# Three homes in turn for the third blocks' left operands, other places for four results, and the next batch's input in four parts

## The chip, the cores and the metric

The kernel runs on one core of a Trainium2 chip. The metric is the time of one execution on the device in microseconds (us); lower is better. The time given is the median of three runs.

## The reference

Routed attention, then a two-layer network with squared ReLU. Cut to what matters:

```python
# q, k, v: (4, 8, 768, 64) float32; centroids: (8, 16, 64)
mask = argmax(q_n . c_n) == argmax(k_n . c_n)          # same cluster
attn = softmax(where(mask, q @ k.T / 8, -1e9)) @ v     # (4, 8, 768, 64)
x = attn.transpose(0, 2, 1, 3).reshape(3072, 512)      # 768 tokens for each of 4 batches
h = x @ w_in                                           # w_in (512, 2048)
g = maximum(h, 0) ** 2
out = g @ w_out                                        # w_out (2048, 512)
```

All is float32. The change touches only the second layer, `g @ w_out`, and the way in which the first layer's input of the next batch is brought in.

## The kernel before

The attention comes first (16 pairs of heads). Then the four batches pass through the network in the order `FEED = (1, 2, 3, 0)`; n = 0 to 3 counts them. Each has an **up** stage (`x @ w_in`, squared) and a **down** stage (`g @ w_out`). From n = 1 on a hand-written order holds on every engine: instructions stand in the engine's queue in the order in which the Python code emits them (`tc.manual_schedule`).

Both layers multiply by the Strassen-Winograd scheme: seven products of half-size blocks in place of eight, with sums and differences of blocks as operands. The products are numbered 1 to 7.

**Up.** `group(i, ...)` forms one of eight groups, seven products of four matmuls each (left 128 columns, right 384). `combine` asks for the products in the order 1, 6, 2, 7, 5, 4, 3. Product 1 needs no sum of x; product 6 needs the sum t2, product 7 needs t3 (which is written over the block `x[0][1]`), product 5 needs t1 and product 4 needs t4. These four sums are made by `x_sums` on VectorE (DVE), from the batch's input `xT` (128 partitions x 3072 floats, 1.5 MB), which for n = 2 and 3 is loaded from the DRAM copy `x_far`. The sums of the weights (`w_sums`, tile `w_s`) are made by GpSimd (POOL), four instructions for each group.

**Down.** A batch's `g` holds 6 blocks of 128 tokens. Four of them (`TWO`) make a full problem for two levels of the scheme. The two others (`THIRD`, the last 128 columns of each half) are half a problem: the third blocks of batch n-1 and of batch n are put side by side, and computed in the down stages of n = 1 and n = 3. Blocks of `g` at `THIRD` are written below as a00, a01 (first half of the tokens) and a10, a11 (second half); each is 128 x 8 x 128. All third blocks and their first-level sums are written to the DRAM tile `g_far` (`store_third`, `third_sums`), and read back by `load_left`.

The class `Down` works through units `(of, j)`: `of` is 0 for the batch's own four blocks, 1 for the pair of third blocks; j is the product of the first level. An odd stage has 14 units, numbered u = 0 to 13:

```
(0,1) (0,4) (1,4) (1,1) (0,5) (1,5) (0,7) (1,7) (0,6) (1,6) (0,2) (1,2) (0,3) (1,3)
```

The even stage (n = 2) has 7, with `of` = 0 only. In each unit:

- `run` issues seven products of the second level (`times`, 8 matmuls of 128x128 each) into two PSUM tiles, `one` and `two`. The right operands are the weights and four precomputed differences in `slot(0..3)`, loaded by `load_right(j)`; each of the four loads waits until TensorE (PE) has read its slot in the unit before.
- `parts` makes, a unit ahead, the sums s and one difference in place (three DVE instructions). A fourth, `sub(x[0][1], x[0][1], s[:, 1])`, stands in the unit itself; the last of the seven products waits for it.
- `combine` turns a unit's products into results, a unit later, in two portions; ScalarE (ACT) copies one product (`copied`). `store` sends finished results to `out` from ACT's DMA queue: results 21 and 22 after product 6, 11 after product 2, 12 after product 3.
- `load_left(j)` brings the third blocks' operands for a later unit, two or four loads of 256 KB on SyncE's (SP) queue.

Where these operands lie is said by `thirds(j)`. Before, j = 4 uses (a01, a11), j = 1 uses (a10, a00), and all the others use (a00, a01) one after the other. The next operands are asked for behind a unit with `of` = 1, for the next such unit. Results lie in tiles of `tp` (`x_t1`, `x_t2`, `x_t4`, those that hold the input's sums in the up stage), in `outp`, and in three pieces of `g` inside a10 and a11 (`third[0..2]`; `third[0]` and `third[1]` are the two halves of a10, `third[2]` the first half of a11). The input of the next batch is loaded whole after unit 1 (`loads()`), and its four sums are made after the last unit (`sums()`), ahead of the last unit's `combine`.

Of the kernel before, what the change touches and what calls it, by code (L numbers as in the profile page):

```python
# [8 lines left out]
F32 = mybir.dt.float32  # L9
# [9 lines left out]
P = 128  # L19
# [6 lines left out]
def kernel(  # L26
# [10 lines left out]
    nc = tc.nc  # L37

    B, H, S, D = q.shape
# [4 lines left out]
    KT = DM // P  # L44
# [21 lines left out]
    loads = att.enter_context(tc.tile_pool(name="loads", bufs=6))  # L66
# [396 lines left out]
    xT = {}  # L463
# [24 lines left out]
    sums = {}  # L488
# [44 lines left out]
    x_far = {b: dram_x.tile([P, KT, S], F32, name=f"x_far{b}") for b in FEED[2:]}  # L533

    H2, F2, M2 = KT // 2, FT // 2, DM // 2

    def sub(out, a, b, eng=nc.vector):
        return eng.tensor_tensor(out=out, in0=a, in1=b, op=ALU.subtract)  # L538

    def x_sums(b):  # L540
        halves = [slice(TB * h, TB * (h + 1)) for h in range(2)]
        x = [[xT[b][:, H2 * g2 : H2 * (g2 + 1), cols] for cols in halves] for g2 in range(2)]
        t1, t2, t4 = (tp.tile([P, H2, TB], F32, name=f"x_t{i}") for i in (1, 2, 4))
        sub(t1, x[0][1], x[0][0])
        yield
        sub(t2, x[1][1], t1)
        yield
        sub(t4, t2, x[1][0])
        yield
        sub(x[0][1], x[1][1], x[0][1])  # L550
        yield x, t1, t2, x[0][1], t4

    def w_sums(i, odd=0):
# [388 lines left out]
    def third_sums(g, n, f):  # L942
        if f < F2 - 1:
            store_third(g, n, f)
        a = block_of(g, f, THIRD)
        third = outp.tile([P, DM], F32, name="third", tag="osb").rearrange("p (j n) -> p j n", j=4)
        plus(third[:, 0], a[1][0], a[1][1])
        sub(third[:, 1], third[:, 0], a[0][0])
        sub(third[:, 2], a[0][0], a[1][0])
        sub(third[:, 3], a[0][1], third[:, 1])  # L950
        return lambda: nc.sync.dma_start(g_far[n][f, :, 3:7], third)

    def times(bank, left, rhs):
        for f in range(F4):
            nc.tensor.matmul(  # L955
                bank, lhsT=left[:, f], rhs=rhs[:, f], start=(f == 0), stop=(f == F4 - 1)
            )

    class Down:
        def __init__(self, b, g, n):  # L960
            self.b, self.g, self.n = b, g, n
# [14 lines left out]

        def thirds(self, j):
            a = blocks(self.g, THIRD)
            return {4: (a[0][1], a[1][1]), 1: (a[1][0], a[0][0])}.get(j, (a[0][0], a[0][1]))

        def load_left(self, j):
            for i, half in ((0, 0), (1, 0), (1, 1), (0, 1)):
# [29 lines left out]
        def find_results(self):  # L1012
            def four(t):
                return t.rearrange("p (i n) -> p i n", i=4)

            def tile(pool, tag):
                return four(pool.tile([P, 4 * P], F32, name="c", tag=tag))

            third = [self.g[:, F4 * i : F4 * (i + 1), 1, THIRD] for i in range(3)]
            if self.n % 2:  # L1020
                self.c = [
                    {11: tile(tp, f"x_t{t}"), 22: third[of]} for of, t in enumerate((1, 2))
                ]
                self.c[0][21], self.c[1][21] = tile(tp, "x_t4"), third[2]
            else:
                self.c = [dict(zip((11, 22, 21), third))]
            for c in self.c:
                c[12] = tile(outp, "osb")
# [35 lines left out]
                    )  # L1064
            self.stores = []

        def run(self, loads, sums):
            first_level(self.g, F2 - 1)
            store_third(self.g, self.n, F2 - 1)
            waiting = None  # L1070
            for u, (of, j) in enumerate(self.units):
                x, s = self.ahead
                y = quarters(right(j))
                copied = spare_tile[:, 4 + u % 2]
                one, two = (
                    bank_tile(4 * P).rearrange("p (i n) -> p i n", i=4) for _ in range(2)
                )
                times(one[:, 0], x[0][0], y[0][0])
                nc.scalar.copy(out=copied, in_=one[:, 0])  # L1079
                self.store()  # L1080
                times(two[:, 0], x[0][1], y[1][0])
                times(two[:, 1], s[:, 1], slot(1))
                times(two[:, 2], x[1][0], slot(2))
                times(two[:, 3], s[:, 0], slot(0))
                times(one[:, 2], x[1][1], slot(3))
                if waiting:
                    next(waiting)
                sub(x[0][1], x[0][1], s[:, 1])
                times(one[:, 1], x[0][1], y[1][1])
                if u + 1 < len(self.units):  # L1090
                    if (k := self.units[u + 1][1]) != j:
# [24 lines left out]

# [74 lines left out]
    x_summed = []  # L1191

    def sum_x(n):
        if n < B:
            x_summed.append(list(x_sums(FEED[n]))[-1])

    for n, b in enumerate(FEED):
        g = gp.tile([P, FT, 2, TB], F32, name="g")
        if n == 0:
            first_up(b, g, Rounding())  # L1200
            first_down(b, g)
            again = nc.values_load(flag[0:1, 0:1], min_val=0, max_val=1)
            with tc.issue_after(last_w_sum[0]):
                sum_x(1)
            manual.enter_context(
                tc.manual_schedule(engines={E.PE, E.DVE, E.Activation, E.Pool, E.SP})
            )
        else:
            stage = Down(b, g, n)
            up(b, g, n, x_summed.pop(), stage.parts)  # L1210
            stage.run(lambda: load_x(n + 1), lambda: sum_x(n + 1))
    manual.close()
    fast.close()

# [189 lines left out]
```

## Time and profile before

| what | value |
|---|---|
| median of 3 runs | 899.92 us (899.64 to 901.14) |
| the profiled execution | 899.35 us |
| its span, first to last instruction | 897.6 us |
| PE busy | 878.8 us, 98% |
| DVE busy | 704.1 us, 78% |
| ACT busy | 389.8 us, 43% |
| POOL busy | 145.7 us, 16% |
| granted TensorE clock | 0.997 |

The stages, from the view of windows (us from the span's start):

| window | stage | PE busy of it |
|---|---|---|
| 516.0 to 606.4 | down, n = 1 | 88.24 of 90.40 |
| 606.4 to 682.7 | up, n = 2 | 73.33 of 76.30 |
| 682.7 to 726.84 | down, n = 2 | 43.16 of 44.14 |
| 726.84 to 801.3 | up, n = 3 | 73.71 of 74.46 |
| 801.3 to 897.6 | down, n = 3, and the end | 87.57 of 96.30 |

In a timeline each row has a start, a duration, the engine, the line, the operation with output <- input, a count, and in brackets the idle time before the row with what ended it. SPq and ACTq are DMA issues. In the chain a row is a start, a duration and what the program's end hung on then.

### The profile page before, as it was taken

The numbers are of one execution on the slowest core, as the hardware profiler recorded it, in microseconds if no ns is written. First come the engines' busy times: TensorE is split into PE (matmuls) and PEld (weight loads), VectorE is DVE, ScalarE is ACT, GpSimd is POOL, SyncE is SP. The second block draws the span as 40 slices with busy tenths as digits, with TensorE's granted clock in tenths as the row PEclk, the third lists the DMA queues.
The fourth block names the chain that finished last, engine by engine and source line by source line (L and its number), as shares of the span: only waits on it lengthen the run. The fifth ranks groups of instructions, "written<-read, shape, count | busy, mean of one in ns | idle before, by whom it ended". The sixth has DMA issues, their size and how long they took to land.

```text
span 897.6 us, 14582 instructions
## 1 busy us (share of the span) xinstructions
PE 878.8 (98%) x5379; PEld 584.6 (65%) x5379; DVE 704.1 (78%) x1271; ACT 389.8 (43%) x621; POOL 145.7 (16%) x168
## 2 busy tenths in 40 slices
PE   9999999999999999999999999998999999999996
PEld 5444444444444455578855599985558975579996
DVE  6798888888888999999566676776667786585875
ACT  5876677776676657630054410003452015530000
POOL 0000100000100257710223100012320052300000
PEclk9999999999999999999999999999999999999998
DMA  6877887777763246236601176662114641126564
GB/s 248 182 188 196 226 239 201 180 210 206 196 147 101 84 164 199 89 106 237 233 35 42 47 231 188 179 180 85 50 53 131 216 142 53 42 71 208 144 188 147
DMA packets 164865, 136.04 MB, mean 152 GB/s; under 512 B 58698, under 2 KB 139186, under 8 KB 164274
## 3 DMA queue, kind: packets, MB, share of 16 engines
q1 hardware_dynamic: 148482, 119.52, 45.5%
q10 hardware_dynamic: 16304, 15.50, 5.6%
q8 instruction: 45, 0.74, 0.3%
q14 instruction: 34, 0.28, 0.1%
HBM read 82.10 MB, written 41.89 MB: 138 GB/s over the span
## 4 chain that ended last, share of the span: by engine, by line
PE 75%; DVE 12%; DMA 9%; issue 2%; SPq 1%; ACT 1%; ACTq 0%; DVEq 0%
PE bank L767 29%; PE sc L441 12%; PE bank L955 9%; PE av_a L475 8%; PE bank L848 5%; DMA g<-g_far 5%; PE av_b L475 4%; PE sc L450 3%; PE sc L329 1%; DVE g L538 1%; DVE l L833 1%; DMA out_dram<-g 1%; DVE spare L833 1%; DVE l L538 1%; PE sc L494 1%
## 5 line engine op out<-in xcount | busy, mean ns | idle before, releaser
L457 ACT ACTIVATE ex<-sc 128x1024 f32<-128x1024 f32 x144 | 144.4, 1026 | 38.3 <-PE sc L441 32.0
L724 DVE TENSOR_TENSOR g<-bank,g 128x384 f32<-128x384 f32 x192 | 102.7, 553 | 72.2 <-PE bank L767 60.4
L441 PE MATMUL sc<-qkT 64*128 64x512 f32 (+1 forms) x768 | 150.6, 484 | 0.0
L743 ACT ACTIVATE g<-g 128x384 f32<-128x384 f32 x122 | 63.3, 519 | 100.3 <-DVE g L724 96.8
L767 PE MATMUL bank<-x_t,w_s 128*128 128x384 f32 x256 | 93.2, 487 | 3.7 <-DVE x_t L538 3.7
L767 PE MATMUL bank<-xT,w_s 128*128 128x384 f32 x256 | 93.4, 487 | 1.1 <-DVE g L724 1.1
L1079 ACT COPY spare<-bank 128x128 f32<-128x128 f32 x35 | 9.3, 265 | 194.6 <-PE bank L955 176.5
L767 PE MATMUL bank<-xT,w_in 128*128 128x384 f32 x256 | 93.3, 487 | 0.0
L441 PEld LDWEIGHTS sc<-qkT 64*128 64x128 f32 x768 | 65.9, 188 | 41.9 <-issue 30.1
L475 PE MATMUL av_a<-ex,v_raw 128*64 128x512 f32 x384 | 85.9, 596 | 0.0
L460 DVE TENSOR_TENSOR total<-total,ex 128x1024 f32<-128x1024 f32 x64 | 78.7, 1229 | 6.5
L558 POOL TENSOR_TENSOR w_s<-w_in 128x256 f32<-128x256 f32 x32 | 26.2, 818 | 325.6 <-PE bank L955 148.9
L955 PE MATMUL bank<-home,l 128*128 128x128 f32 x560 | 74.1, 275 | 1.0 <-DMA home<-w_far 1.0
L767 PEld LDWEIGHTS bank<-x_t,w_s 128*128 128x128 f32 x256 | 48.5, 190 | 38.3 <-issue 3.7
L767 PEld LDWEIGHTS bank<-xT,w_s 128*128 128x128 f32 x256 | 48.3, 190 | 36.1 <-issue 3.3
L767 PEld LDWEIGHTS bank<-xT,w_in 128*128 128x128 f32 x256 | 48.3, 190 | 33.7 <-DVE g L538 0.6
L161 POOL TENSOR_TENSOR w_in<-w_in,w_raw 128x512 int32<-128x512 int32 x16 | 22.0, 1376 | 295.0 <-DVE w_in L153 278.4
L955 PEld LDWEIGHTS bank<-home,l 128*128 128x128 f32 x560 | 68.1, 192 | 1.2 <-DVE g L538 1.1
L744 ACT ACTIVATE g<-g 128x384 f32<-128x384 f32 x122 | 63.8, 523 | 3.9
L475 PEld LDWEIGHTS av_a<-ex,v_raw 128*64 128x64 f32 x384 | 26.1, 137 | 51.0 <-issue 49.3
L450 PE MATMUL sc<-rows 64*128 64x512 bf16 (+1 forms) x360 | 59.0, 323 | 0.3 <-DVE sums_t L503 0.3
L955 PE MATMUL bank<-home,g 128*128 128x128 f32 x416 | 54.9, 275 | 0.0
(181 smaller groups left out, 1401.7 us busy)
## 6 DMA issues: line engine op xcount, KB each, us to landing
home<-w_far SPq DMA_DIRECT2D x92, 256.0 KB
g<-g_far SPq DMA_DIRECT2D x48, 256.0 KB
words<-flat SPq DMA_DIRECT2D x26, 384.0 KB
w_raw<-in_moe_w_in_dram SPq DMA_DIRECT2D x16, 512.0 KB
w_raw<-in_moe_w_out_dram SPq DMA_DIRECT2D x16, 512.0 KB
w_far<-home SPq DMA_DIRECT2D x28, 256.0 KB
v_raw<-in_v_dram SPq DMA_DIRECT2D x16, 384.0 KB
rb<-far_r SPq DMA_DIRECT2D x32, 192.0 KB
```

The source lines that it names most:

```text
L441: nc.tensor.matmul(sc[i][:, e, cols], lhsT=qkT[pair][rows, NCH + c], rhs=qkT[pair][rows, n.start // P : n.stop // P], start=first, stop=no ...
L450: nc.tensor.matmul(sc[i][:, e, cols], lhsT=ohT[pair][rows, 1, c * P : (c + 1) * P], rhs=ohT[pair][rows, 0, columns(i)], start=first, stop= ...
L457: nc.scalar.activation(out=ex[i], in_=sc.pop(i), func=ACT.Exp, scale=SCALE)
L460: eng.tensor_tensor(out=out, in0=a, in1=b, op=ALU.add)
L475: nc.tensor.matmul(bank[D * e : D * (e + 1), 0 : n.stop - n.start], lhsT=raw_v[pair][:, e, c], rhs=ex[i][:, e, cols], start=c == 0, stop=c ...
L558: nc.gpsimd.tensor_tensor(out=s1, in0=a[1][0], in1=a[1][1], op=ALU.add)
L724: nc.vector.tensor_tensor(out=out, in0=bank, in1=to, op=ALU.add)
L743: nc.scalar.activation(out=to, in_=to, func=ACT.Relu)
L744: nc.scalar.square(to, to)
L767: nc.tensor.matmul(bank, lhsT=operands[j][0][:, kk], rhs=operands[j][1][:, kk], start=(kk == 0), stop=(kk == H2 - 1),)
L848: nc.tensor.matmul(bank, lhsT=left[j][:, f], rhs=right(j)[:, f], start=(f == 0), stop=(f == F2 - 1),)
L955: nc.tensor.matmul(bank, lhsT=left[:, f], rhs=rhs[:, f], start=(f == 0), stop=(f == F4 - 1))
```

## The change

- **Homes.** In the odd stages a new tile `extra` (three pieces of 128 x 8 x 128) takes the place of the finished input (tag `x1`). Products 5 and 6 take `extra[0]` and `extra[1]`, products 7 and 2 take a00 and a01, product 3 takes a10 and a11; product 1's loaded half goes to `extra[2]`.
- **Load times.** Operands 4, 1 and 5 are loaded in unit 0; then, behind the units (1,1), (1,5), (1,7) and (1,2), those of products 7, 6, 2 and 3 (`LATER`). Nothing is loaded behind (1,6).
- **Results.** In the odd stages: 11 of the own blocks to `x_t2`, 21 to `third[0]`, 22 to `third[1]`; of the third blocks 11 to `x_t4`, 21 to `x_t1`, 22 to `third[2]`.
- **Input.** The next batch's input comes in four loads of 384 KB (`LOADS`): in the even stage behind the units 1 to 4, in an odd stage behind the units 9, 10 (two) and 12.
- **Sums.** The order of the sums is t1, t2, t3, t4 (t3 and t4 change places). t1 is made behind the last unit but one, t2 and t3 behind the last, t4 after the last `combine`.

```diff
@@ x_sums
         sub(t2, x[1][1], t1)
         yield
+        sub(x[0][1], x[1][1], x[0][1])
+        yield
         sub(t4, t2, x[1][0])
-        yield
-        sub(x[0][1], x[1][1], x[0][1])
         yield x, t1, t2, x[0][1], t4
@@ ahead of class Down
+    LATER = {1: 7, 5: 6, 7: 2, 2: 3}
+    LOADS = ({1: (0,), 2: (1,), 3: (2,), 4: (3,)}, {9: (0,), 10: (1, 2), 12: (3,)})
@@ Down.thirds
-            return {4: (a[0][1], a[1][1]), 1: (a[1][0], a[0][0])}.get(j, (a[0][0], a[0][1]))
+            return {
+                4: (a[0][1], a[1][1]), 1: (self.extra[:, 2], a[0][0]), 3: (a[1][0], a[1][1]),
+                7: (a[0][0], a[0][1]), 2: (a[0][0], a[0][1]),
+            }.get(j, (self.extra[:, 0], self.extra[:, 1]))
@@ Down.find_results
                 self.c = [
-                    {11: tile(tp, f"x_t{t}"), 22: third[of]} for of, t in enumerate((1, 2))
+                    {11: tile(tp, "x_t2"), 21: third[0], 22: third[1]},
+                    {11: tile(tp, "x_t4"), 21: tile(tp, "x_t1"), 22: third[2]},
                 ]
-                self.c[0][21], self.c[1][21] = tile(tp, "x_t4"), third[2]
+                self.extra = xp.tile([P, 3, F2, P], F32, name="extra", tag="x1")
@@ Down.run
-                    if of and j != 4 and (k := next((k for o, k in self.units[u + 1 :] if o), None)):
-                        self.load_left(k)
+                    if of and j in LATER:
+                        self.load_left(LATER[j])
...
                 if u == 0:
                     store = third_sums(self.g, self.n, F2 - 1)
+                    self.find_results()
                     if self.n % 2:
                         self.load_left(4)
+                        self.load_left(1)
                     store()
                     if self.n % 2:
-                        self.load_left(1)
-                    self.find_results()
-                elif u == 1:
-                    loads()
+                        self.load_left(5)
                 if waiting:
                     next(waiting, None)
                 waiting = self.combine(of, j, one, two, copied)
-                if u + 1 == len(self.units):
-                    sums()
+                to_end = len(self.units) - 1 - u
+                for kk in LOADS[self.n % 2].get(u, ()):
+                    load_x(self.n + 1, kk)
+                if to_end == 1:
+                    sum_x(self.n + 1, 1)
+                elif to_end == 0:
+                    sum_x(self.n + 1, 2)
             list(waiting)
+            sum_x(self.n + 1, 1)
             self.store()
@@ load_x, sum_x
-    def load_x(n):
+    def load_x(n, kk):
         if n < B:
-            xT[FEED[n]] = xp.tile([P, KT, S], F32, name="xT", tag="x1")
-            nc.sync.dma_start(xT[FEED[n]], x_far[FEED[n]])
+            b = FEED[n]
+            if b not in xT:
+                xT[b] = xp.tile([P, KT, S], F32, name="xT", tag="x1")
+            nc.sync.dma_start(xT[b][:, kk], x_far[b][:, kk])
...
-    def sum_x(n):
+    def sum_x(n, steps):
         if n < B:
-            x_summed.append(list(x_sums(FEED[n]))[-1])
+            if n not in x_summed:
+                x_summed[n] = [x_sums(FEED[n])]
+            for _ in range(steps):
+                x_summed[n].append(next(x_summed[n][0]))
```

For the first batch, before the hand-written order begins, all four sums are still made at once, in the new order.

More of the change, by code (lines that the diff above doesn't have):

```diff
@@ L1065, in store, with run @@
             self.stores = []
-        def run(self, loads, sums):
+        def run(self):
             first_level(self.g, F2 - 1)
@@ L1184 @@
     wtp = spare_tile = four_r = None
-    def load_x(n):
+    def load_x(n, kk):
         if n < B:
-            xT[FEED[n]] = xp.tile([P, KT, S], F32, name="xT", tag="x1")
-            nc.sync.dma_start(xT[FEED[n]], x_far[FEED[n]])
-    x_summed = []
-    def sum_x(n):
+            b = FEED[n]
+            if b not in xT:
+                xT[b] = xp.tile([P, KT, S], F32, name="xT", tag="x1")
+            nc.sync.dma_start(xT[b][:, kk], x_far[b][:, kk])
+    x_summed = {}
+    def sum_x(n, steps):
         if n < B:
-            x_summed.append(list(x_sums(FEED[n]))[-1])
+            if n not in x_summed:
+                x_summed[n] = [x_sums(FEED[n])]
+            for _ in range(steps):
+                x_summed[n].append(next(x_summed[n][0]))
     for n, b in enumerate(FEED):
@@ L1203 @@
             with tc.issue_after(last_w_sum[0]):
-                sum_x(1)
+                sum_x(1, 4)
             manual.enter_context(
@@ L1209 @@
             stage = Down(b, g, n)
-            up(b, g, n, x_summed.pop(), stage.parts)
-            stage.run(lambda: load_x(n + 1), lambda: sum_x(n + 1))
+            up(b, g, n, x_summed.pop(n)[-1], stage.parts)
+            stage.run()
     manual.close()
```

## The prediction

> **What bounds it now.** The page first: PE is busy 878.8 us of a span of 897.6, so at most 18.8 us are to be had, start and end included. I then read PE's waits, PE's timeline for the rows with an idle time in brackets, and for each of them DVE's and SP's timelines and the chain. PE's waits:
>
> ```profile
> PE bank L767 <- DVE x_t L538: 3.7, 2, 3.0
> PE bank L955 <- DVE g L538: 2.4, 2, 1.3
> ...
> PE bank L955 <- DMA home<-w_far: 1.0, 1, 1.0
> PE bank L955 <- DMA g<-g_far: 0.9, 2, 0.6
> ```
>
> All of these lie where the change works: the input's sums (L538 into x_t), the third blocks' operands (g), and a slot load (home) that stands behind the whole input in SP's queue. PE's timeline places them, four in the first odd stage, two in the even one, two in the last:
>
> ```profile
> 585.92 1.13 PE L955 MATMUL bank<-w_out,g 128*128 128x128 f32 x8 [0.30 <-DMA g<-g_far]
> ...
> 591.91 1.16 PE L955 MATMUL bank<-w_out,g 128*128 128x128 f32 x8 [1.29 <-DVE g L538]
> ...
> 600.78 1.13 PE L955 MATMUL bank<-w_out,g 128*128 128x128 f32 x8 [0.57 <-DMA g<-g_far]
> ...
> 610.83 1.53 PE L767 MATMUL bank<-x_t,w_s 128*128 128x384 f32 x4 [2.97 <-DVE x_t L538]
> ...
> 703.54 1.13 PE L955 MATMUL bank<-home,l 128*128 128x128 f32 x8 [0.98 <-DMA home<-w_far]
> ...
> 729.05 1.53 PE L767 MATMUL bank<-x_t,w_s 128*128 128x384 f32 x4 [0.75 <-DVE x_t L538]
> ...
> 876.05 1.16 PE L955 MATMUL bank<-w_out,g 128*128 128x128 f32 x8 [1.08 <-DVE g L538]
> ...
> 884.78 1.13 PE L955 MATMUL bank<-w_out,g 128*128 128x128 f32 x8 [0.42 <-SPq L1215]
> ```
>
> The second is DVE being late, and DVE is late because it waited for operands; the third is the same for the last operands; the fourth is t2, whose place x_t2 is still being stored:
>
> ```profile
> 571.60 0.69 DVE L833 TENSOR_TENSOR l<-g 128x512 f32<-128x512 f32 x1 [3.12 <-DMA g<-g_far]
> ...
> 585.00 0.69 DVE L833 TENSOR_TENSOR l<-g 128x512 f32<-128x512 f32 x1 [1.84 <-DMA g<-g_far]
> ...
> 599.85 1.20 DVE L833 TENSOR_TENSOR l<-g 128x512 f32<-128x512 f32 x1 [3.29 <-DMA g<-g_far]
> ...
> 609.72 0.96 DVE L538 TENSOR_TENSOR x_t<-xT,x_t 128x768 f32<-128x768 f32 x1 [2.56 <-DMA out_dram<-c]
> ```
>
> The chain says what the operands of product 3 hung on: a store of results, then SP's issue, then the load.
>
> ```profile
> 589.31 5.91 DMA out_dram<-g
> 595.24 0.37 SPq L985
> ...
> 595.66 4.17 DMA g<-g_far
> ```
>
> **What the Trainium skill says.** "GPSIMD Engine Reference", section Specifications: POOL's SBUF interfaces are shared with DVE, and contend with DVE instructions that have two SBUF inputs. The trace agrees: beside POOL's w_s sums (719.10 to 723.2) four 512-element adds took 1.07, 1.10, 1.21 and 1.10 us, alone 0.69; adds with a PSUM input stay at 0.42. "DMA: Bandwidth & Descriptors", section Queues, rings and completion order: SP's and ACT's DMAs share the same 16 engines, each serving the queues in turn. The trace agrees: with stores in the same microseconds a load landed 6.2 us after issue (877.92 to 884.09), with few of them 4.2. The same page, section Anatomy of one DMA: a DMA's wait is served on the issuing engine, so what stands behind it in that queue waits too; SP's four issues of 592.60 took 4.19 us, two behind a wait, where a free four take 2.03.
>
> **The change, stage by stage.** A unit is 56 matmuls in 6.25 us (starts 0.893 apart per product); T11 is the start of unit 11, and so on.
>
> *n = 1.* T11 is 584.56. Without waits T12 = 590.81, T13 = 597.06, up starts at 603.31. Before it started at 606.40, and its product 6 at 610.83 in place of one product (1.29) later, 607.69. To be had: 3.1 + 3.1 = 6.2 us.
>
> Operands 5, 7, 6 and 2 now come one third-block unit earlier: 2, issued at 578.0 to 580.2 and landed at 585.0, will be issued behind unit 7, at 565.5, where operands 6 were (landed at 571.6). DVE no longer waits at 571.60 and 585.00. Followed through its queue, bounded by PE (the sub of unit 9 can start 1.99 us after T9 = 572.06, as in unit 1), product 6's combine ends at 586.5 instead of 590.06, the sub of unit 11 at 588.2, and PE wants it at T11 + 5.36 = 589.9. Cover 1.7 us, so 0.30 and 1.29 go.
>
> Operands 3 are late next. Their new home (a10, a11) holds results that must have been stored. These stores were issued at 588.84 to 591.5; now, with the combine 3.6 us earlier, at 586.0 to 587.9, ahead of the slot loads instead of among them. The chain has such stores at 3.60 us (874.31) and 5.91 (589.31), the longer among other loads; I take the shorter, so 591.5 for the last. SP issues the slot loads at 587.5 to 590.2 (PE sets them) and the four operand loads at 590.6 to 592.5; at 4.2 to 4.9 us they land at about 597, the third of them (which DVE wants first) at 596.3. PE needs the last at T13 + 0.89 = 597.95. So 0.57 goes.
>
> But DVE now has t1 between. From 596.3: parts 1.93, plus about 0.8 beside POOL's first group of sums, which starts at T12 + 4.5 = 595.3; the rest of a combine 1.1; t1 1.03; the next combine's first portion 1.12; the sub 0.6: 602.9. PE wants it at T13 + 5.36 = 602.42, so about 0.6 us of wait, a new one. Behind it DVE does 1.0 of combine, then t2 (1.0 to 1.36 beside POOL): 605.0 to 605.4. Up starts at 603.9, product 6 wants t2 at 605.2. Its place x_t2 is free: result 11 of the own blocks is stored a unit earlier. Product 6 starts at 605.4. t3 and t4 (by 606.7 and 610.2, the last combine between) are wanted at 607.9 and 610.5. **Gain 610.83 - 605.4 = 5.4 us.** Bounds: 6.2 if POOL costs nothing; 2.9 if operands 3 land as late as before (599.85 + 5.8 of DVE + 0.9 + 1.3 = 607.9).
>
> *The input's loads.* Four issues in place of one, 0.4 to 0.5 us each on SP. The first waits in SP's queue for PE to leave unit 9 (`extra` is read until 578.3); behind it stand only the next two and the slot loads of unit 11, which wait for PE until 587.5 anyway: nothing. The fourth stands behind operands 3 and ahead of slots that are wanted 75 us later: nothing. In units 9 and 10, 1.1 MB of input take the place of 1 MB of operands 2. If the engines ran full, operands 3 would land up to 1 us later; that is in the range. In unit 0, 1 MB of operands 5 takes the place of 1.5 MB of input, behind operands 4 and 1: nothing.
>
> *n = 2.* The wait at 703.54 exists because 1.5 MB stand between two units' slot loads (issued at 694.03). With 384 KB there the first slot lands near 700, wanted at 702.4: **1.2 us** with the restart. At the end, before: product 6 began 0.9 late, and another 0.3 us of small waits on x_t3 and PSUM. Now t1 is in the unit before. DVE there is full: the combine of product 6 ends 3.12 us after T6 (beside POOL), t1 1.03, then 1.12 and 0.6: 5.95, and PE wants the sub at 5.36: 0.64 us of new wait; t2 is then in time by about 0.1. **Net 0.5**, between -0.6 (both sums at 1.4) and 1.2. Together 1.7.
>
> *n = 3.* No next input. As in n = 1, waits of 1.08 and 0.42, with restarts and two rows of 0.1 to 0.2 in units 9 and 11, come to 2.2 us of PE; operands 3 land at about 880.5 with T13 = 881.7, 1.4 early. Then the tail: before, DVE ended at 892.3, 2 us behind PE (about 890.3), its queue still late from 884.09. Now PE ends at 888.1, and only the last 128x256 add (0.42) with its wait follows: 888.8. The two stores and the end follow as before. **Gain 3.5 us**; 0 if operands 3 land as before.
>
> *n = 0.* The order of t3 and t4 changes; PE has no wait there: nothing.
>
> Sum: 5.4 + 1.7 + 3.5 = 10.6 us. The profiled execution took 899.35 (span 897.6 and 1.75 around it), 0.57 below the median; a difference carries over, so 899.92 - 10.6 = **889.3 us**. All that is to be had, 6.2 + 2.5 + 3.7, would give 887.5.
>
> **Rivals.** *The last operands stay late* (chance 0.17). For it: the load chain of a store, an issue and 4 to 6 us; the input in units 9 and 10 fills the DMA engines. Against: the stores leave 3 us earlier. Then 2.9 + 1.2 + 0 = 4.1 us of gain: 895.8. *No early operands* (0.04): if `extra` or the new place of results is tied to a later event than I read, SP's in-order queue gives the early loads back; about 899.9. *The store ahead of operands 3 decides* (0.05), the slower side: product 3's operands overwrite results, so they can't leave before these stores have landed. With s us from the last store's issue (587.9; in n = 3 872.7) to its landing, 0.5 for the next issue and 4.2 for the load, the third load lands at 592.6 + s, and up's product 6 follows 9.1 later: n = 1 gains 9.1 - s, n = 3 6.7 - s, n = 2 its 1.7. The change is slower from s = 8.8 on; the slowest store seen took 5.9. With s = 11: 904.4.
>
> **Numbers.** The forecast has 0.74. Below 0.2% (1.8 us, about what a measurement can tell from no change) nothing counts as faster. The forecast and the late operands are faster: 0.91; no early operands 0.04 the same; the slower rival 0.05. The range 887.3 to 894.5 holds the forecast's bounds and reaches towards the late operands.
>
> **What would show it.** Right: no operand wait on DVE at units 8 and 10; one left before unit 13's parts, ending near 596.5; product 6 of up near 605.4; no wait on home<-w_far; new PE waits of 0.5 to 1 us on the sub of the last unit in n = 1 and 2; DVE's last add within 1 us of PE's end. Wrong: operands 3 landing after 599, or waits on l<-g in earlier units.

## The result, and the profile after

The changed kernel takes 891.42 us (median of 6 runs, 889.51 to 893.32), the kernel before 899.78 beside it (6 runs): a ratio of 0.9907, with a 95% interval of 0.9889 to 0.9924. The gain is 8.4 us; 10.6 were forecast, and the time lies 2.1 above the predicted 889.3, inside the range. The profiled execution took 891.05 us, its span is 889.3, and the granted clock 0.997 as before. One run of n3_early_sums_first (below) took 915.07 us, in a slow state with a granted clock of 0.948, and is left out of its median and ratio.

The page's first lines, after:

```profile
span 889.3 us, 14583 instructions
...
PE 876.6 (99%) x5379; PEld 584.1 (66%) x5379; DVE 703.8 (79%) x1271; ACT 389.9 (44%) x621; POOL 145.7 (16%) x168
```

PE has the same number of matmuls, and of the 8.3 us of span 6.1 were PE's idle time (18.8 before, 12.7 now). The other 2.2 are in its busy time (878.8 before), in part because the first matmuls behind a wait are longer in PE's timeline (1.13 to 1.16 us for eight, where 1.06 is usual) and there are fewer waits now. PE's waits after (us in total, times, the longest):

```profile
PE bank L955 <- DMA g<-g_far: 1.1, 2, 0.8
...
PE bank L955 <- DVE g L538: 0.4, 1, 0.4
...
PE bank L955 <- DVE home L538: 0.3, 1, 0.3
```

The wait on x_t (3.7) and the one on home<-w_far (1.0) are gone, the one on DVE's g went from 2.4 to 0.4; the last operands (g<-g_far) still cost PE 1.1 (0.9 before), and the sub of the last unit in n = 2 is new. PE's timeline places what is left:

```profile
598.58 1.13 PE L955 MATMUL bank<-w_out,g 128*128 128x128 f32 x8 [0.80 <-DMA g<-g_far]
...
603.65 1.16 PE L955 MATMUL bank<-w_out,g 128*128 128x128 f32 x8 [0.37 <-DVE g L538]
604.65 1.46 PE L767 MATMUL bank<-xT,w_in 128*128 128x384 f32 x4
605.94 1.45 PE L767 MATMUL bank<-x_t,w_s 128*128 128x384 f32 x4
...
720.23 1.16 PE L955 MATMUL bank<-w_out,home 128*128 128x128 f32 x8 [0.30 <-DVE home L538]
...
722.52 1.45 PE L767 MATMUL bank<-x_t,w_s 128*128 128x384 f32 x4
...
876.15 1.13 PE L955 MATMUL bank<-w_out,g 128*128 128x128 f32 x8 [0.33 <-DMA g<-g_far]
...
880.69 1.06 PE L955 MATMUL bank<-w_out,g 128*128 128x128 f32 x8
```

605.94 and 722.52 are product 6 of the up stages; neither row has a bracket now. These two rows cut the gain into parts that can be set against the prediction's. With the first matmul of the down stage n = 1 at 515.78 before and 515.43 after:

| stretch | before | after | gain |
|---|---|---|---|
| start to down n = 1 | 515.78 | 515.43 | 0.35 |
| to product 6 of up, n = 2 | 95.05 | 90.51 | 4.54 |
| to product 6 of up, n = 3 | 118.22 | 116.58 | 1.64 |
| to the end of the span | 168.55 | 166.78 | 1.77 |
| sum | 897.6 | 889.3 | 8.30 |

DVE's rows at the units where it waited for operands before (571.60, 585.00, 599.85), then the first row of the last unit's parts in n = 3 and DVE's last row:

```profile
568.05 0.69 DVE L833 TENSOR_TENSOR l<-extra 128x512 f32<-128x512 f32 x1
...
581.07 0.69 DVE L833 TENSOR_TENSOR l<-g 128x512 f32<-128x512 f32 x1
...
597.69 0.93 DVE L833 TENSOR_TENSOR l<-g 128x512 f32<-128x512 f32 x1 [4.54 <-DMA g<-g_far]
...
875.49 0.69 DVE L833 TENSOR_TENSOR l<-g 128x512 f32<-128x512 f32 x1 [4.30 <-DMA g<-g_far]
...
883.29 0.42 DVE L833 TENSOR_TENSOR c<-bank,c 128x256 f32<-128x256 f32 x1
```

The first two have no bracket: the early homes do what they should. The third and the fourth wait longer than any before, since DVE arrives early at operands that have not come. That alone is no loss (DVE waits longer here than before, and both stages are shorter all the same); what it costs is on PE, 0.80 and 0.33, and at the end: DVE's last add ends at 883.71, PE's last matmul at 881.75, so DVE still stands 2 us behind PE as it did before.

The chain, after, at both places (start, duration, what the end hung on):

```profile
591.61 5.99 DMA g<-g_far
...
869.20 6.19 DMA g<-g_far
```

Before, the load in this place took 4.17 in n = 1 and 6.08 in n = 3. The prediction took 4.2 to 4.9 in n = 1; this is the main number of it that fell, and the experiments go after it.

### The profile page after: what moved, and what is told of

Its sections match the earlier page's. It is cut to its first block, busy times and chain, and to the rows that moved or that the text cites. A ratio compares the mean times of both kernels' runs of the same rounds, so it can differ in the third digit from the quotient of the medians.

```text
span 889.3 us, 14583 instructions
## 1 busy us (share of the span) xinstructions
PE 876.6 (99%) x5379; PEld 584.1 (66%) x5379; DVE 703.8 (79%) x1271; ACT 389.9 (44%) x621; POOL 145.7 (16%) x168
## 4 chain that ended last, share of the span: by engine, by line
PE 85%; DVE 9%; DMA 3%; issue 2%; ACT 1%; SPq 0%; ACTq 0%; DVEq 0%
PE bank L767 30%; PE bank L955 18%; PE sc L441 12%; PE av_a L475 8%; PE bank L848 5%; PE av_b L475 4%; PE sc L450 3%; PE sc L329 1%; DMA g<-g_far 1%; DVE spare L833 1%; DVE c L833 1%; PE sc L494 1%; DMA qkT<-words 1%; DVE g L724 1%; DVE g L538 1%
## 5 line engine op out<-in xcount | busy, mean ns | idle before, releaser
L767 PE MATMUL bank<-x_t,w_in 128*128 128x384 f32 x128 | 46.5, 486 | 0.0
```

Source lines behind the costliest of these rows:

```text
L767: nc.tensor.matmul(bank, lhsT=operands[j][0][:, kk], rhs=operands[j][1][:, kk], start=(kk == 0), stop=(kk == H2 - 1),)
```

## The experiments

For all of them, lengths of the stages from PE's timeline, from the start of the first matmul to the end of the last, in us. D1, D2, D3 are the down stages of n = 1, 2, 3; U2 and U3 the up stages between; the tail is from PE's last matmul to the end of the span. Free of waits an odd down stage takes 87.71 and an up stage 72.41 (the shortest seen).

| kernel | D1 | U2 | D2 | U3 | D3 | tail | median us | ratio to before, 95% interval |
|---|---|---|---|---|---|---|---|---|
| before | 90.79 | 75.61 | 45.15 | 73.73 | 89.97 | 7.2 | 899.78 | |
| changed | 89.38 | 72.41 | 44.50 | 72.41 | 88.28 | 7.5 | 891.42 | 0.9907 (0.9889 to 0.9924) |
| homes_only | 88.70 | 73.81 | 48.34 | 73.72 | 88.76 | 7.4 | 894.15 | 0.9934 (0.9913 to 0.9955) |
| input_only | 90.49 | 73.84 | 44.50 | 72.41 | 90.39 | 6.9 | 897.88 | 0.9979 (0.9969 to 0.9989) |
| ops3_early | 90.05 | 72.41 | 44.50 | 72.41 | 87.71 | 5.8 | 890.06 | 0.9896 (0.9875 to 0.9917) |
| even_whole | 89.38 | 72.41 | 44.97 | 72.41 | 88.96 | 6.3 | 892.86 | 0.9927 (0.9905 to 0.9949) |
| after_again | 89.11 | 72.41 | 44.51 | 72.41 | 88.51 | 7.6 | 891.33 | 0.9906 (0.9878 to 0.9935) |
| n3_early_sums_first | 88.74 | 73.43 | 43.93 | 73.33 | 87.71 | 6.0 | 889.87 | 0.9897 (0.9862 to 0.9931) |
| no_slots3 | 88.95 | 72.41 | 44.51 | 72.41 | 87.71 | 6.0 | 889.58 | 0.9886 (0.9857 to 0.9915) |
| even_whole_2 | 89.11 | 72.41 | 45.74 | 72.40 | 88.03 | 7.8 | 892.61 | 0.9921 (0.9892 to 0.9951) |
| n3_early | 89.38 | 72.41 | 44.51 | 72.41 | 87.71 | 6.0 | 889.96 | 0.9900 (0.9882 to 0.9918) |
| n3_early_n1_one | 89.75 | 72.41 | 44.51 | 72.41 | 87.71 | 5.9 | 890.06 | 0.9896 (0.9879 to 0.9913) |

The first four experiments ran beside one set of runs of the kernel before (median 899.34), the next four beside another (899.33), the last two beside a third (899.28). All edits are against the changed kernel.

### The homes alone (homes_only)

The homes, load times and places of results stay; the input comes whole and its sums are made at the end, in the old order.

```diff
...
-    LOADS = ({1: (0,), 2: (1,), 3: (2,), 4: (3,)}, {9: (0,), 10: (1, 2), 12: (3,)})
+    LOADS = ({1: (slice(0, KT),)}, {9: (slice(0, KT),)})
...
-                if to_end == 1:
-                    sum_x(self.n + 1, 1)
-                elif to_end == 0:
-                    sum_x(self.n + 1, 2)
+                if to_end == 0:
+                    sum_x(self.n + 1, 4)
             list(waiting)
-            sum_x(self.n + 1, 1)
```

> The new homes, the new places of the results and the new load times alone; the input comes whole (behind unit 1 in the even stage, behind unit 9 in the odd one, since its place holds the operands until then) and its four sums are made behind the last unit in the old order. My theory: the homes carry the odd stages' gain (4.5 us in n = 1 and 1.8 in n = 3 by the two profiles), the input in parts and the early sums only that of n = 2 (1.6). So this runs at about 893.0 us, with the wait on home<-w_far (about 1.0 us) back in n = 2 and operand waits gone from units 8 and 10. Rival: the sums' new place frees t2 in n = 1 (the wait of 2.97 us before), and the homes only remove 0.3 and 1.3 us twice: then about 896.

Measured: 894.15, a gain of 5.2, where the theory had 893.0 and the rival 896. The profiled execution (897.91) was the slowest of its seven runs, so its stages are read for their waits and not added up. PE's timeline:

```profile
606.80 1.53 PE L767 MATMUL bank<-x_t,w_s 128*128 128x384 f32 x4 [0.84 <-DVE x_t L538]
...
701.39 1.77 PE L955 MATMUL bank<-home,l 128*128 128x128 f32 x8 [2.55 <-DMA home<-w_far]
...
728.52 1.53 PE L767 MATMUL bank<-x_t,w_s 128*128 128x384 f32 x4 [0.74 <-DVE x_t L538]
```

D1 is 2.09 shorter than before, more than in the changed kernel (1.41): here t1 doesn't stand ahead of the last unit's sub, and PE doesn't wait for that. Of the 2.97 us that PE waited for x_t in n = 1, 0.84 are left although the sums stand where they stood. So the homes and the places of the results alone take most of that wait: DVE is less late from the operands, and its row of t2 has no wait for the store out of x_t2 any more (2.56 before). The next experiment shows that the sums alone take as much of U2 (1.8 us in both). The two parts overlap, and their gains don't add up. The waits of n = 2 stay: they are the input's part.

### The input alone (input_only)

The four parts and the new sums stay (in the odd stages the loads stand behind units 1 to 4, since `extra` is not there); homes, load times and results are as before.

```diff
-    LOADS = ({1: (0,), 2: (1,), 3: (2,), 4: (3,)}, {9: (0,), 10: (1, 2), 12: (3,)})
+    LOADS = ({1: (0,), 2: (1,), 3: (2,), 4: (3,)},) * 2
...
+            return {4: (a[0][1], a[1][1]), 1: (a[1][0], a[0][0])}.get(j, (a[0][0], a[0][1]))
...
-                    if of and j in LATER:
-                        self.load_left(LATER[j])
+                    if of and j != 4 and (k := next((k for o, k in self.units[u + 1 :] if o), None)):
+                        self.load_left(k)
...
```

> The old homes and old places of results; the input in four parts (behind units 1 to 4 in every stage) and its sums in the new order and at the new places. My theory: in n = 1 t2 still waits for the store of result 11 of the third blocks, whose place it takes, so nothing is gained there; n = 2 gains 1.6 us: about 898.2 us, with PE's wait on x_t in n = 1 still near 3 us. Rival: the earlier sums bring most of the change's gain: 894 or less.

Measured: 897.88, a gain of 1.5. PE's timeline:

```profile
592.30 1.16 PE L955 MATMUL bank<-w_out,g 128*128 128x128 f32 x8 [1.03 <-DVE g L538]
...
609.80 1.53 PE L767 MATMUL bank<-x_t,w_s 128*128 128x384 f32 x4 [1.20 <-DVE x_t L538]
...
873.73 1.16 PE L955 MATMUL bank<-w_out,g 128*128 128x128 f32 x8 [1.60 <-DVE g L538]
```

The total came as expected, one detail didn't: the wait on x_t in n = 1 fell to 1.20 where I expected it to stay near 3. U2 is 1.8 shorter with the new order and places of the sums alone; t2 still waits for the store out of its place, 1.54 us for 2.56. PE's waits on DVE at the operands stay (1.03 and 1.60 for 1.29 and 1.08), and the last unit's sub in n = 1 has a new one of 0.80. D2 and U3 have the changed kernel's lengths, so what n = 2 gained comes from the input's part, and what n = 3 gained from the homes (D3 and tail 97.3 here, 97.2 before).

### The last operands earlier, in both odd stages (ops3_early)

Of product 3's four operand loads three are asked for behind unit 10, ahead of the slot loads; only the one whose place is stored last stays where it was.

```diff
-        def load_left(self, j):
-            for i, half in ((0, 0), (1, 0), (1, 1), (0, 1)):
+        def load_left(self, j, which=((0, 0), (1, 0), (1, 1), (0, 1))):
+            for i, half in which:
...
-                        self.load_left(LATER[j])
+                        self.load_left(LATER[j], *[((1, 0),)] * (LATER[j] == 3))
...
+                if self.n % 2 and u == 10:
+                    self.load_left(3, ((1, 1), (0, 0), (0, 1)))
```

> The changed kernel, with three of the four loads of product 3's operands issued behind unit 10, ahead of unit 12's slot loads; only the one that overwrites the third blocks' result 22 stays behind them. My theory: what is left in n = 1 and 3 hangs on the landing of these operands (DVE waits for them until 597.69 in n = 1 and 875.49 in n = 3, 6 us after issue, since they queue behind 1 MB of slot loads). With 0.25 MB left there they land some 3 us earlier, PE's waits of 0.80, 0.37 and 0.33 go, and DVE's last add ends within 1 us of PE: 3 us less, about 888.4. Rival 1: DVE's work in the last units bounds them anyway: within 0.5 us of 891.4. Rival 2: SP's queue, now waiting for the stores of unit 8's results ahead of the slot loads, delays those: a new wait on home<-w_far and 892 or more.

Measured: 890.06, a gain of 1.4 for the 3 expected. In n = 3 all came: D3 is 87.71 with no wait, the tail 5.8. In n = 1 the load's place was paid for by another wait. SP's timeline, then PE's:

```profile
580.03 7.10 SPq L993 DMA_DIRECT2D g<-g_far  x3
587.18 5.44 SPq L914 DMA_DIRECT2D home<-w_far  x4
```

```profile
593.04 1.13 PE L955 MATMUL bank<-home,l 128*128 128x128 f32 x8 [0.97 <-DMA home<-w_far]
...
603.98 1.16 PE L955 MATMUL bank<-w_out,g 128*128 128x128 f32 x8 [0.87 <-DVE g L538]
```

The trace has 16 completion signals for each DMA, and it has landed with the last. Two of the three loads wait for stores: those issued at 579.20 and 580.54 landed at 585.15 and 586.70, and SP goes on at 585.17 and 586.72. So the three issues take SP 7.10 us, and the third operand load goes out at 586.77, just ahead of the slots. The first slot load, at 587.18, is hardly later than in the changed kernel (587.09), but the operands stand ahead of it, the last of them until 592.24. It lands at 592.91, 5.73 us after its issue where the changed kernel has 3.65, and PE waits 0.97 for it. (The four slot issues take 5.44 us for 3.00 because the fourth goes out at 592.30 only, behind the landing of the third operand load: the two signal on the same semaphore.) D1 is 0.67 longer than in the changed kernel. In n = 3 the same loads stand in the same order and cost nothing: the store that the third load waits for took 2.86 us there (6.16 in n = 1), and all three had landed at 865.30, ahead of the first slot load (865.46). There is no next input beside them in n = 3; that this is the reason wasn't tested.

### The even stage's input whole again (even_whole, even_whole_2)

```diff
-    LOADS = ({1: (0,), 2: (1,), 3: (2,), 4: (3,)}, {9: (0,), 10: (1, 2), 12: (3,)})
+    LOADS = ({1: (slice(0, KT),)}, {9: (0,), 10: (1, 2), 12: (3,)})
```

> The changed kernel with the input whole behind unit 1 in the even stage (n = 2), in parts as before in the odd one. My theory: the wait on home<-w_far at unit 3 of n = 2 (0.98 us, 1.2 with the restart) comes back: about 892.6. Rival: it does not, since the wait belonged to something else in the old order: 891.4.

> The input whole behind unit 1 of the even stage, once more, beside the changed kernel on the same chip. In the first run PE's wait on home<-w_far in n = 2 was 0.23 us, in the kernel with the homes alone 2.55, in the kernel before 0.98: the wait depends on the execution. If the four parts are worth their 1.2 us, this is slower than the changed kernel by 0.5 to 2 us; if not, by under 0.3.

Measured: 892.86 and, with the changed kernel beside it on the same chip (891.33), 892.61, so 1.3 us for the four parts in n = 2, against the 1.2 of the prediction. The intervals of the ratios overlap; the stage is clearer. D2 is 44.97 and 45.74 where the changed kernel has 44.50 and 44.51, and PE's timeline of the second has the old wait back:

```profile
698.64 1.13 PE L955 MATMUL bank<-home,l 128*128 128x128 f32 x8 [1.00 <-DMA home<-w_far]
```

The size of this wait varies between executions: 0.23 and 1.00 in two of this same kernel, 0.98 before and 2.55 in homes_only, where the input also comes whole behind unit 1.

### The changed kernel again (after_again)

No edit.

> The changed kernel once more, beside the others of this group on the same chip: 891.4 us, 0.99 of the kernel before.

Measured: 891.33. In this execution the third load of n = 1 landed 1.2 us sooner than in the first one: at 596.42, 4.74 us after its issue, with the same loads ahead of it. By the completion signals 0.9 of that is the last signal alone: the fifteenth came at 596.40 here and at 596.69 in the first execution, the sixteenth at 596.42 and 597.60. DVE's timeline shows what the earlier landing is worth:

```profile
596.51 1.27 DVE L833 TENSOR_TENSOR l<-g 128x512 f32<-128x512 f32 x1 [3.53 <-DMA g<-g_far]
597.82 1.10 DVE L538 TENSOR_TENSOR l<-l,g 128x512 f32<-128x512 f32 x1
```

The first two operations of the parts take 1.27 and 1.10, where the first execution had 0.93 and 0.69: they now run beside POOL's first group of sums (595.01 to 598.36 here, 595.18 to 598.07 in the first execution). This is the contention that the Trainium skill describes ("GPSIMD Engine Reference", section Specifications), and which the prediction priced at 0.8 us in all. D1 is shorter by 0.27 only.

### The last operands earlier in n = 3 alone, and t1, t2 and t3 behind the last sub (n3_early_sums_first)

In n = 3 the loads as in ops3_early; t1, t2 and t3 are made behind the last unit's own sub, so that t1 no longer stands ahead of it.

```diff
...
-                        self.load_left(LATER[j])
+                        early = self.n == B - 1 and LATER[j] == 3
+                        self.load_left(LATER[j], *[((1, 0),)] * early)
...
+                if u + 1 == len(self.units):
+                    sum_x(self.n + 1, 3)
                 if waiting:
...
-                if to_end == 1:
-                    sum_x(self.n + 1, 1)
-                elif to_end == 0:
-                    sum_x(self.n + 1, 2)
+                if self.n == B - 1 and u == 10:
+                    self.load_left(3, ((1, 1), (0, 0), (0, 1)))
```

> The changed kernel with two further edits: three of the four loads of product 3's operands behind unit 10 in n = 3 alone (in n = 1 the slots came late by it), and t1, t2 and t3 in the last unit, behind the sub that PE waits for and ahead of the rest of the combine of the unit before. My theory: in n = 3 2.3 us less, as in the run with the early loads in both stages; the new waits of 0.37 us in n = 1 and 0.30 us in n = 2 are the price of t1 ahead of that sub, so they go, and t2 is still in time (by 0.7 us, or just if POOL's sums slow it): 0.5 and 0.4 us less. Together about 3 us under the changed kernel, 888.2. Rival: t1 and t2 behind the sub are late for up's product 6, which then waits as long as the sub did: only n = 3 gains, 889.1.

Measured: 889.87, the rival's 889.1 rather than the theory's 888.2. The waits on the sub are gone (D1 0.64 shorter, D2 0.57), and come back a few us later in the up stages, 1.0 and 0.9 longer. PE's timeline:

```profile
611.17 1.53 PE L767 MATMUL bank<-x_t,w_in 128*128 128x384 f32 x4 [0.41 <-DVE x_t L538]
...
728.11 1.53 PE L767 MATMUL bank<-x_t,w_in 128*128 128x384 f32 x4 [0.42 <-DVE x_t L538]
```

Product 4 now waits for t4. DVE's timeline has no free time between the last operands and t4, so this order of its work moved the wait and didn't remove it.

### Without the slot loads of product 3 (no_slots3)

The four slot loads of product 3 are left out in the odd stages, so the last two units multiply by the slots of product 2. The kernel leaves out part of the computation, and serves only to time the loads behind.

```diff
-                    if (k := self.units[u + 1][1]) != j:
+                    if (k := self.units[u + 1][1]) != j and not (self.n % 2 and k == 3):
                         load_right(k)
```

> The changed kernel without the four slot loads of product 3 in the odd stages, which leaves out part of the computation: units 12 and 13 of n = 1 and 3 multiply by product 2's differences instead. It measures what the 1 MB of slot loads ahead of operands 3 costs their landing. SP then issues the operands as soon as the stores of unit 9's results have landed. My theory: these stores land near 590 (n = 1), so the issue moves little, by about 1 us, but the landing comes 4.2 us after the issue, not 6.1: DVE starts near 595 instead of 597.7 in n = 1, and near 872.5 instead of 875.5 in n = 3, and n = 3 gains its 2.3 us. Rival: the landing is long because of the operands' own 512-byte pieces and the stores on ACT's queue, and the slots don't matter: landing 6 us after issue still, gain under 1 us.

Measured: 889.58. In n = 3 the operands come before DVE asks (its row has no bracket), D3 is 87.71 and the tail 6.0. In n = 1 the third load lands 4.0 us after its issue; the chain, SP's timeline and DVE's:

```profile
593.41 4.01 DMA g<-g_far
```

```profile
588.02 6.50 SPq L993 DMA_DIRECT2D g<-g_far  x4
```

```profile
597.51 0.98 DVE L833 TENSOR_TENSOR l<-g 128x512 f32<-128x512 f32 x1 [3.14 <-DMA g<-g_far]
...
871.98 0.69 DVE L833 TENSOR_TENSOR l<-g 128x512 f32<-128x512 f32 x1
```

Yet the landing is hardly earlier than in the changed kernel (597.42 for 597.60): SP's four issues take 6.50 us, because the second waits for a store. The trace's completion signals give both times: the last signal of the store issued at 588.86 comes at 592.87, and SP goes on at 592.88. So with the slots out of the way the store is what the last operands of n = 1 hang on, 4.0 us of it; the theory, which had DVE start near 595 in n = 1, missed that (597.51).

The same signals show where the changed kernel's 6 us go:

| us | last slot load landed | operand loads landed | third load: issued, took |
|---|---|---|---|
| before, n = 1 | 595.04 | 596.63, 598.63, 599.83, 600.65 | 595.66, 4.17 |
| before, n = 3 | 880.75 | 881.61, 882.55, 884.00, 884.64 | 877.92, 6.08 |
| changed, n = 1 | 593.30 | 594.74, 596.10, 597.60, 598.44 | 591.61, 5.99 |
| changed, n = 3 | 871.01 | 872.72, 874.44, 875.39, 876.01 | 869.20, 6.19 |
| no_slots3, n = 1 | none | (one gone early) 596.23, 597.42, 598.26 | 593.41, 4.01 |

Loads of SP's queue land one behind the other, about 1.2 us apart. The Trainium skill ("DMA: Bandwidth & Descriptors", section Queues, rings and completion order) says that each engine takes a queue's descriptors in ring order, though not that they complete in that order; in the table they landed in order in every row. The time from issue to landing is then mostly not the load's own: it is what stands ahead of it.

The rival is ACT's stores in the same microseconds. The view of the DMA queues tells the two apart, over the time from the third load's issue to its landing. The time of a queue is its share of the 16 engines times this window:

| third load | window us | SP's queue: MB, share, time | ACT's queue: MB, share, time |
|---|---|---|---|
| before, n = 1 | 4.17 | 0.82, 67.8%, 2.8 us | 0.26, 19.1%, 0.8 us |
| before, n = 3 | 6.08 | 1.18, 68.9%, 4.2 us | 0.25, 12.6%, 0.8 us |
| changed, n = 1 | 5.99 | 1.58, 83.8%, 5.0 us | 0.26, 12.7%, 0.8 us |
| changed, n = 3 | 6.19 | 1.40, 75.2%, 4.7 us | 0.26, 12.3%, 0.8 us |
| after_again, n = 1 | 4.74 | 1.23, 88.2%, 4.2 us | 0.26, 16.2%, 0.8 us |
| no_slots3, n = 1 | 4.01 | 0.81, 70.4%, 2.8 us | 0.26, 20.1%, 0.8 us |
| n3_early (below), the one load left, n = 3 | 3.50 | 0.44, 39.6%, 1.4 us | 0.26, 22.6%, 0.8 us |

The stores take the same 0.8 us in every row. What differs is SP's own queue. (Its share can include loads behind the third one, where an engine was ahead of the others.)

### The last operands earlier in n = 3 alone (n3_early)

n3_early_sums_first without its move of the sums: in n = 3 three loads behind unit 10, all else as in the changed kernel.

```diff
+                        early = self.n == B - 1 and LATER[j] == 3
+                        self.load_left(LATER[j], *[((1, 0),)] * early)
...
+                if self.n == B - 1 and u == 10:
+                    self.load_left(3, ((1, 1), (0, 0), (0, 1)))
```

> The changed kernel with three of the four loads of product 3's operands behind unit 10, ahead of the slot loads, in n = 3 alone; the sums stay where the change put them. My theory: n = 3 loses its wait on operands (0.3 to 0.6 us) and DVE ends within 1 us of PE, 2.3 us less; n = 1 and 2 as in the changed kernel: 889.1. Rival: nothing beyond the 1.3 us that the two earlier kernels with such loads showed in the median, 890.0, since part of what DVE saves is lost in the last stores.

Measured: 889.96. D1 to U3 are the changed kernel's, D3 is 87.71 and the tail 6.0. The chain and DVE's timeline in n = 3:

```profile
865.67 4.21 DMA out_dram<-g
...
869.96 3.50 DMA g<-g_far
```

```profile
873.49 0.69 DVE L833 TENSOR_TENSOR l<-g 128x512 f32<-128x512 f32 x1 [2.45 <-DMA g<-g_far]
...
881.39 0.42 DVE L833 TENSOR_TENSOR c<-bank,c 128x256 f32<-128x256 f32 x1
```

The one load left hangs on a store (4.21) and then takes 3.50, with slots ahead of it but no other operands. DVE's last add now ends 0.8 us behind PE (881.81, PE 881.03). Against the changed kernel it is 1.4 us lower in the medians, of other runs, and the intervals overlap: the whole time is the rival's 890.0 and not the theory's 889.1. The stage is clear (0.6, and 1.5 us of tail), and so over all traces: D3 and the tail together take 95.3 to 96.2 us in the five executions with these loads as the change has them (changed, after_again, homes_only, even_whole, even_whole_2) and 93.5 to 93.8 in the five where they come earlier or have no slots ahead.

### And one of the loads earlier in n = 1 (n3_early_n1_one)

```diff
+                        late = [((1, 0),)] if self.n == B - 1 else [((0, 0), (1, 0), (0, 1))]
+                        self.load_left(LATER[j], *late * (LATER[j] == 3))
...
+                if self.n % 2 and u == 10:
+                    self.load_left(3, ((1, 1), (0, 0), (0, 1))[: 3 if self.n == B - 1 else 1])
```

> The same, and in n = 1 the one load that overwrites no result (second half of a11) behind unit 10, the three others behind the slots. My theory: 0.25 MB less behind the slots, so n = 1's operands land about 0.9 us earlier, PE's wait on them (0.2 to 0.8 us) goes; but DVE's sums then fall beside POOL's first group and cost up to 1 us more, so the sub of the last unit gains little: 0.3 us under n3_early, 888.8. Rival: the engines are full with the input's three parts at that time, so the load pushes the slots of unit 12: a wait on home<-w_far, and 0.5 us over n3_early.

Measured: 890.06, no gain; a miss. PE's wait for the operands in n = 1 is gone, and D1 is 0.37 longer all the same. PE's timeline:

```profile
595.23 1.16 PE L955 MATMUL bank<-home,l 128*128 128x128 f32 x8 [0.18 <-DMA home<-w_far]
...
604.87 1.16 PE L955 MATMUL bank<-w_out,g 128*128 128x128 f32 x8 [0.60 <-DVE g L538]
```

A slot is late now, as the rival said, and the sub later than before. In n = 1 the stores, the slots, the operands and the input share the same 10 us, and three orders of the loads gave three places of the wait with D1 between 89.1 and 90.1.

## Why the prediction was right, and where it was off

- **n = 1, the early operands: right.** The rows at 568.05 and 581.07 have no bracket. The combine of product 6 ended at 586.1 (586.5 forecast), its stores were issued by 587.5 (587.9), and SP issued the four operand loads from 590.19 to 592.66 (590.6 to 592.5). The forecast used the clock of the kernel before, and the stage began 0.35 earlier here, so in the stage's own time these came as forecast.
- **n = 1, the last operands: mis-sized.** The third load was to land at 596.3, "at 4.2 to 4.9 us" after its issue. It took 5.99 and landed at 597.60, in the stage's own time 1.65 later than forecast. This is the term that was wrong. The 4.2 came from a load whose slots had landed when it was issued (595.04, then 595.66, in the table), with two operand loads ahead; now three of the four slot loads were still under way at its issue (591.61) beside the two operand loads. The prediction had the other row, 877.92 to 884.09, in hand, and read it as "with stores in the same microseconds", the 4.2 as "with few of them". That reading was wrong: the stores moved 0.25 and 0.26 MB in the two windows, SP's own queue 1.18 and 0.82. Its doubt about the input in units 9 and 10 isn't the reason either, since n = 3 has no input and took 6.19. Not all of the 5.99 is the queue: the last completion signal alone came 0.9 after the fifteenth, and after_again had 4.74. The late load also makes PE wait 0.80 where none was forecast.
- **n = 1, DVE's queue behind it: right in kind, with an offset.** The sub of unit 13 was late by 0.37 (0.6 forecast). From the third landing to the sub's end the forecast had 6.6 us, and it was 6.0, because the operands came at the end of POOL's group and the 0.8 us beside POOL was not paid in full; product 6 then had no wait, where 0.2 was forecast. So a landing 1.65 too late cost 0.9: 4.54 of the 5.4 came. In after_again the landing was 1.0 sooner in the stage's time, the contention was paid (6.7 us to the sub's end), and the stage was shorter by 0.27 only. So, by this one pair of executions, a landing on time would not have brought the 0.9 back in full.
- **n = 2: right.** 1.64 of 1.7. The wait on home<-w_far is gone (even_whole_2: 1.3 us when it is put back), the new wait on the sub was 0.30 (0.64 forecast; the four terms given for it add up to 5.87 and not to 5.95, so 0.1 less).
- **n = 3: the same term.** 1.77 of 3.5. The third load took 6.19 and landed 81.9 us after the stage's start, where 80.1 follows from the forecast's 880.5. D3 is 0.57 longer than free of waits (0.33 of it in the bracket), and DVE kept its lag of 2 us to the end: the tail is 7.5, where 6.0 follows from the forecast. With the loads early, n3_early has D3 and tail of 93.7, against 97.2 before: 3.4 us, 0.1 short of the forecast. So the late landing accounts for this part.
- **n = 0:** nothing was forecast; 0.35 lies ahead of the first down stage. In the twelve traces that stage starts between 515.09 and 516.82, so 0.35 is within what executions differ by.
- **The sum:** 0.9 of n = 1 and 1.7 of n = 3 missing, 0.35 more ahead: 8.3 for 10.6.
- **The rivals.** "The last operands stay late" was half true: later than forecast, 2.2 us earlier than before (DVE's row at 597.69 for 599.85). "No early operands" fell with the rows at 568.05 and 581.07. "The store ahead of operands 3 decides" has its mechanism in the trace: in the changed kernel SP's second load of n = 1 goes out at 591.18, 0.1 us behind the landing of the store issued at 587.01 (591.10), and in no_slots3 and n3_early the operands hang on it. But its s was 4.0 to 4.2 in all three, far from the 8.8 from which it would have made the change slower.

**What stays open.** No run removed both waits that PE still has in n = 1 (0.80 and 0.37). Another place for the results of product 6, so that no store stands ahead of the last operands, was not tried. How much of the landing is the 1 MB of slots and how much the two operand loads in front isn't separated: no_slots3 takes away the slots, but there the store also lets the first operand load go 4 us ahead. Why the last completion signal is late in some executions is open too.

## What to carry to other kernels

A load's time from issue to landing is no constant to be copied from another row: count what stands ahead of it in its queue, and take the time from the landing of the last of these (0.6 to 2.0 us later here). Leave room for a spread: the same load took 4.74 and 5.99 in two executions. When operands are to come earlier, look for the last ones in the row, whose home is freed last; here 2.6 us of the 10.6 were missing at them (0.9 and 1.7), while the operands before them cost PE nothing any more. A wait that lies in a stretch where one engine has no free time (DVE between the last operands and t4) moved when the order of its work was changed (n3_early_sums_first). That it goes when what feeds it comes sooner isn't shown: 1.2 us sooner brought 0.3 in after_again.

## What the runs showed of the hardware

- Loads of 256 KB on one queue landed 0.6 to 2.0 us apart, 1.2 in the mean of the table. From issue to landing the third operand load took 4.7 to 6.2 us behind slots and two operand loads, 4.2 behind two operand loads (before, n = 1), 4.0 behind one, and 3.5 where slots alone were ahead.
- The last of the 16 completion signals of one DMA is at times far behind the others. The store of 586.58 had its first signal at 588.27, its fifteenth at 588.72 and its last at 590.13, 1.4 us later; the third operand load of the changed kernel's n = 1 had 0.9 us there (596.69 and 597.60). What held the last signal wasn't settled.
- The same 512-element DVE add took 0.69 us alone and 0.93 to 1.27 beside POOL's sums; in after_again an operand that landed 1.2 us sooner, beside these sums, brought 0.3.
